# Removing the idle TensorE products ahead of the first work of an attention and MLP kernel

## The chip, the cores and the metric

The kernel runs on one core of one Trainium2 chip. A core has five engines with their own instruction streams: TensorE (PE in the profile, with its weight loads as PEld), VectorE (DVE), ScalarE (ACT), GpSimd (POOL) and SyncE (SP), which here does nothing but issue DMAs. The metric is the device time of one execution in microseconds, as the median of several runs.

## The reference

The work is attention with normed queries and keys, followed by an MLP with an unusual activation. In short:

```python
# q, k, v: (8, 12, 448, 64) float32; g_q, g_k: (64,)
q_n, k_n = rmsnorm(q, g_q), rmsnorm(k, g_k)       # x / sqrt(mean(x*x) + 1e-6) * g
scores = q_n @ k_n.T / sqrt(64)
attn   = softmax(scores)
x      = (attn @ v), heads side by side           # (3584, 768)
h      = x @ w_in                                 # w_in  (768, 2048), float64
out    = (h - tanh(h)) @ w_out                    # w_out (2048, 768), float64
```

The weights come in as float64; the kernel reads them as pairs of 32-bit words and rounds them to float32 itself.

## The kernel before, in words

**Attention in steps.** A step is one batch and one pair of heads, so there are 8 x 6 = 48 steps. For a step, `load` fetches q, k and v; `squares` (ACT, L137 and L138) squares q and k; `norm` (L147 to L149) sums the squares on DVE and takes the power -1/2 on POOL; `norm_q` (L428, DVE) scales q; `turn` (L434 to L452) transposes the keys on TensorE (L439), copies them out with the gain `g_col` to `kT` (L441, ACT), transposes the normed queries (L445) and copies them to `qT` (L449, ACT). `scores` (L518) multiplies kT by qT in blocks of 32 keys (L532), and ACT takes the exponential (L538) with the key's norm as its scale. `totals` (L654) sums the probabilities, `last_values` and `values` (L581, L631) multiply them by v, and `divide` (L706) divides. Queries and keys of a step are held in two buffers each, so the load of step s+2 waits until step s has been read: the q load for `norm_q`, the k load for the key transposes.

**The stages are laid out as a pipeline by hand.** `first_slot(s)` (L971) issues one slot: for step s the totals, values and division, for step s+1 the scores, for step s+2 the transposes, for step s+3 the squares and norms, and the load of step s+4. It runs for s from -3 to 5, so the first slots have only the front part of the pipeline. The schedule is manual: each engine works strictly in the order in which the program issues, and waits by semaphores where an operand is not there. The slots after that (`early_slot`, `slot`) mix attention with products of the MLP of an earlier batch.

**The weights.** Each slot also handles a piece of the weights: a DMA of 768 KB (`weight_load`, L279 and L283) into a staging area, two ACT operations (L71, L72), three on DVE (L78, L79, L82) and one on POOL (L90); later the pieces are combined on DVE (L342). MLP products (L761) work on two halves in each dimension with seven products in place of eight; for the first batch the second layer is done plainly (L926). All DMAs but two go through SP's queue, in program order.

**The score banks.** In the first slots five PSUM banks called `sc` are used in turn for scores and query transposes, and three called `mm` for the rest.

**The idle products.** `keep_busy` (L128 to L132) issues a number of matmuls of the identity by half of itself, into a PSUM bank that nobody reads. It is called three times at the very start: 12 products once the identity is made (L1401), 18 between the key transposes and the query transposes of step 0 (L443), and 5 after the query transposes of step 0 (L451). The profile shows each product as two matmul records and two weight loads, under L132.

Of the kernel before, what the change touches and what calls it, by code (L numbers as in the profile page):

```python
# [9 lines left out]
F32 = mybir.dt.float32  # L10
# [5 lines left out]
PSUM = bass.MemoryType.PSUM  # L16
# [76 lines left out]
def fetch(nc, name, t, pair, in_order=False):  # L93

    S = pair.shape[1]
    P = 128
    KF, KR = S // P, S % P
    if name == "q":
        if in_order:
            for h in range(2):  # L100
                nc.sync.dma_start(out=t[:, h], in_=pair[h].rearrange("(c p) d -> p c d", c=NCH))
            return
        nc.sync.dma_start(
            out=t.rearrange("p h c d -> p h (c d)"), in_=pair.rearrange("h (p c) d -> p h (c d)", c=NCH)
        )
        return
    full, rest = pair[:, : KF * P].rearrange("h (p c) d -> h p c d", c=KF), pair[:, KF * P :]
    if name == "v":
        last = t[:, :, KF]
    elif in_order:  # L110
        last = t[:, KF]
    if in_order:
        for h in range(2):
            to = t[:, h, :KF] if name == "v" else t[:, :KF, h]
            nc.sync.dma_start(out=to, in_=pair[h, : KF * P].rearrange("(c p) d -> p c d", p=P))
    elif name == "v":
        nc.sync.dma_start(
            out=t[:, :, :KF].rearrange("p h c d -> p h (c d)"), in_=full.rearrange("h p c d -> p h (c d)")
        )
    else:  # L120
        last = t[:, KF]
        for h in range(2):
            nc.sync.dma_start(out=t[:, :KF, h], in_=full[h])
    for r in range(2):
        nc.sync.dma_start(out=last[r * KR : (r + 1) * KR], in_=rest.rearrange("h p d -> p h d"))


def keep_busy(nc, ident, bank, count):  # L128

    half = ident.shape[0] // 2  # L130
    for _ in range(count):
        nc.tensor.matmul(bank[:, 512 - half :], lhsT=ident, rhs=ident[:, :half], start=True, stop=True)  # L132


def squares_of(nc, sq, n, q, k):

    nc.scalar.activation(n.rearrange("p c h d -> p (c h) d"), q.rearrange("p a b d -> p (a b) d"), AF.Square)  # L137
    nc.scalar.activation(sq, k.rearrange("p a b d -> p (a b) d"), AF.Square)  # L138


def norm_of(nc, rr, sq, n, neg_half):

    D = sq.shape[2]
    for i, x in ((1, n.rearrange("p c h d -> p (c h) d")), (0, sq)):
        rows = x.shape[0]
        r = rr[:rows, i]
        nc.vector.reduce_sum(r, x, axis=AX.X)  # L147
        nc.vector.tensor_scalar(out=r, in0=r, scalar1=1.0 / D, scalar2=1e-6, op0=ALU.mult, op1=ALU.add)  # L148
        nc.gpsimd.tensor_tensor(out=r, in0=r, in1=neg_half[:rows], op=ALU.pow)  # L149


def bounded_path(tc, ctx, q, k, v, moe_w_in, moe_w_out, out, g_col, ident, ones, half_ones, neg_half, early):
# [17 lines left out]
    nc = tc.nc  # L170
    B, H, S, D = q.shape
    DFF, DM = moe_w_out.shape
    P = 128
# [35 lines left out]
    banks = {name: [ps.tile([P, 512], F32, name=f"{name}{i}") for i in range(n)] for name, n in (("sc", 5), ("mm", 3))}  # L209
# [224 lines left out]
    def turn(s, tk, tq):  # L434

        rr, n = normed.pop(s), early["n"]
        kn = loaded.pop(("k", s))
        for c in range(NCH):
            nc.tensor.transpose(tk[:, c * P : (c + 1) * P], kn[:, c].rearrange("p h d -> p (h d)"), ident)  # L439
        kT = qkp.tile([P, S], F32, name="kT")  # L440
        nc.scalar.mul(kT, tk[:, :S], g_col)  # L441
        if s == 0:
            keep_busy(nc, ident, banks["mm"][0], 18)  # L443
        for c in range(NCH):
            nc.tensor.transpose(  # L445
                tq[:, c * CP : (c + 1) * CP], n[:, c].rearrange("p h d -> p (h d)"), ident[:CP, :CP]
            )
        qT = qkp.tile([P, S], F32, name="qT")
        nc.scalar.copy(out=qT, in_=tq[:, :S])  # L449
        if s == 0:  # L450
            keep_busy(nc, ident, banks["mm"][0], 5)  # L451
        turned[s] = rr, kT, qT  # L452


# [516 lines left out]
    def first_slot(s):  # L971
# [4 lines left out]
        if has(s + 2):  # L976
            turn(s + 2, mm_bank(), sc_bank())
# [61 lines left out]
    def slot(s):  # L1039
# [24 lines left out]
        if blocks:  # L1064
            norm_blocks(s + 2)
        elif has(s + 2):
            turn(s + 2, sc_bank(), sc_bank())
# [276 lines left out]
@with_exitstack  # L1344
def kernel(
    ctx: ExitStack,
    tc: tile.TileContext,
    q: bass.AP,
    k: bass.AP,
    v: bass.AP,  # L1350
    g_q: bass.AP,
    g_k: bass.AP,
    moe_w_in: bass.AP,
    moe_w_out: bass.AP,
    out: bass.AP,
):

    nc = tc.nc
    B, H, S, D = q.shape
    P = 128
    CP = S // NCH
    scale = 1.0 / float(D) ** 0.5

    consts = ctx.enter_context(tc.tile_pool(name="consts", bufs=1))

    rows = consts.tile([P, 4 * NCH * D], F32, name="rows")  # L1370
    early = {
        "q": rows[:CP, 2 * NCH * D :].rearrange("p (h c d) -> p h c d", h=2, c=NCH),
        "k": rows[:, : 2 * NCH * D].rearrange("p (c h d) -> p c h d", c=NCH, h=2),
        "sum": rows[:, : 2 * S].rearrange("p (h s) -> p h s", h=2),
        "n": consts.tile([CP, NCH, 2, D], F32, name="n"),
        "sq": consts.tile([P, 2 * NCH, D], F32, name="sq"),
        "rr": consts.tile([P, 2, 2 * NCH], F32, name="rr"),
    }
    gcol = consts.tile([D, 2], F32, name="gcol")
    most = consts.tile([1, 1], F32, name="most")  # L1380
    flag = consts.tile([1, 1], I32, name="flag")
    warm = consts.tile([1, 1], F32, name="warm")
    g_col = consts.tile([P, 1], F32, name="g_col")
    ident = consts.tile([P, P], F32, name="ident")
    ones = consts.tile([P, D // 2], F32, name="ones")
    half_ones = consts.tile([P, 2, D // 2], F32, name="half_ones")
    neg_half = consts.tile([P, 2 * NCH], F32, name="neg_half")
    with tc.manual_schedule(), tc.tile_pool(name="g", bufs=1) as gp:
        grow = gp.tile([1, 2, D], F32, name="grow")
        prod = gp.tile([1, D], F32, name="prod")  # L1390
        nc.scalar.dma_start(out=grow[:, 0, :], in_=g_q[None, :])
        nc.scalar.dma_start(out=grow[:, 1, :], in_=g_k[None, :])
        for name, src in (("q", q), ("k", k)):
            fetch(nc, name, early[name], src[0, 0:2])
        for i, src in enumerate((g_q, g_k)):
            nc.sync.dma_start(out=gcol[:, i : i + 1], in_=src[:, None])
        nc.vector.memset(warm, 0.0)
        nc.scalar.activation(warm, warm, AF.Exp)
        make_identity(nc, ident)
        with tc.tile_pool(name="idle", bufs=1, space=PSUM) as idle:  # L1400
            keep_busy(nc, ident, idle.tile([P, 512], F32, name="idle"), 12)  # L1401
        nc.vector.memset(neg_half, -0.5)
        nc.vector.memset(ones, 1.0)
        nc.vector.memset(half_ones, 0.0)
        for i in range(2):
            nc.vector.memset(half_ones[i * D : (i + 1) * D, i], 1.0)
        nc.vector.tensor_tensor(out=prod, in0=grow[:, 0, :], in1=grow[:, 1, :], op=ALU.mult)
        nc.vector.tensor_tensor(out=prod, in0=prod, in1=prod, op=ALU.mult)
        nc.vector.tensor_reduce(out=most, in_=prod, op=ALU.max, axis=AX.X)
        nc.vector.tensor_scalar(  # L1410
            out=flag, in0=most, scalar1=(SCORE_MAX / (scale * D)) ** 2, scalar2=None, op0=ALU.is_le
        )
        squares_of(nc, early["sq"], early["n"], early["q"], early["k"])
        norm_of(nc, early["rr"], early["sq"], early["n"], neg_half)
    bounded = nc.values_load(flag[0:1, 0:1])

    def make_g_col():
        for base in (0, D):
            nc.vector.tensor_scalar(
                out=g_col[base : base + D], in0=gcol[:, 0:1], scalar1=gcol[:, 1:2], scalar2=scale,  # L1420
                op0=ALU.mult, op1=ALU.mult,
            )

    early["g_col"] = make_g_col
    with tc.If(bounded) as cmp:
        with ExitStack() as arm, tc.manual_schedule():
            bounded_path(tc, arm, q, k, v, moe_w_in, moe_w_out, out, g_col, ident, ones, half_ones, neg_half, early)
    with cmp.Else():
        with ExitStack() as arm:
            make_g_col()  # L1430
            general_path(tc, arm, q, k, v, moe_w_in, moe_w_out, out, g_col, ident, neg_half)
# [30 lines left out]
```

## Time and profile before

| What | Value |
|---|---|
| Runs | 1392.99, 1393.02, 1395.43 us; median 1393.02 |
| Profiled execution, its own time | 1394.76 us |
| Its span in the trace | 1392.9 us |
| PE busy | 1366.8 us (98%) |
| PE weight loads busy | 1142.7 us (82%) |
| DVE busy | 942.1 us (68%) |
| POOL busy | 562.1 us (40%) |
| ACT busy | 504.3 us (36%) |
| DMA moved | 249.91 MB, 179 GB/s on average |
| L132 records on PE | 24 into the bank `idle`, 46 into the bank `mm` |

The span is the time from the first to the last instruction in the trace; the execution's own time also holds what lies around it. A row of the timeline gives start and length in us, the engine, the line of the program, the operation, and what it writes and reads; in brackets stands how long the engine was idle before it and who released it. Matmuls overlap, so the length of one record is longer than the step from one to the next. A share of busy time is an average over stages with different limits.

### The profile page before, as it was taken

How to read it: one execution, taken by the hardware profiler on the slowest of the kernel's cores; microseconds unless marked ns; L12 is line 12 of the kernel's file. 1: busy time of each engine (PE TensorE's matmuls, PEld its weight loads, DVE VectorE, ACT ScalarE, POOL GpSimd, SP SyncE). 2: the span in 40 equal slices, each digit the busy share in tenths (PEclk: the TensorE clock that was granted, in tenths of full speed). 3: DMA queues.
4: the chain of work that ended last, by engine and by line, in shares of the span. 5: the costliest groups of instructions: out<-in, count | busy, mean ns of one | idle time of the engine just before them, and what ended most of it. 6: DMA issues, size and time to landing. Idle time of an engine off the chain costs nothing.

```text
span 1392.9 us, 30057 instructions
## 1 busy us (share of the span) xinstructions
PE 1366.8 (98%) x11910; PEld 1142.7 (82%) x11910; DVE 942.1 (68%) x1545; ACT 504.3 (36%) x1147; POOL 562.1 (40%) x345
## 2 busy tenths in 40 slices
PE   9979899999999999999999999999999999999997
PEld 6458764478898898889889988988988998899997
DVE  3999978856876688567866668657885677633311
ACT  5855555233422433334332343224333234301100
POOL 3656655314542346225544236423552355402300
PEclk9999999999999999999999999999999999999999
DMA  6888789857666666766666666667667666366663
GB/s 157 184 215 214 230 257 235 219 168 180 183 165 168 174 171 173 179 158 190 173 158 183 181 162 182 178 157 181 169 165 177 177 177 188 100 188 184 191 192 89
DMA packets 367657, 249.91 MB, mean 179 GB/s; under 512 B 281748, under 2 KB 309780, under 8 KB 367508
## 3 DMA queue, kind: packets, MB, share of 16 engines
q1 hardware_dynamic: 367504, 247.90, 66.7%
q8 instruction: 96, 1.57, 0.5%
q14 instruction: 53, 0.43, 0.1%
q10 hardware_dynamic: 4, 0.00, 0.0%
HBM read 214.40 MB, written 33.42 MB: 178 GB/s over the span
## 4 chain that ended last, share of the span: by engine, by line
PE 91%; DVE 5%; DMA 2%; issue 1%; ACT 1%; POOL 0%; SPq 0%; DVEq 0%; POOLq 0%; ACTq 0%
PE mm L761 66%; PE sc L532 9%; PE sc L593 6%; PE mm L926 4%; DMA w_f<-w_out 1%; PE sc L581 1%; PE sc L631 1%; DVE w_out L82 1%; DVE w_out L79 1%; PE mm L132 1%; DMA w_raw<-in_moe_w_out_dram 1%; DVE w_out L342 1%; PE mm L631 1%; DVE rs L659 1%; DVE w_out L78 0%
## 5 line engine op out<-in xcount | busy, mean ns | idle before, releaser
L761 PE MATMUL mm<-xT,w_f 128*128 128x224 f32 x1392 | 278.5, 354 | 1.7 <-DVE s L817 1.7
L761 PEld LDWEIGHTS mm<-xT,w_f 128*128 128x128 f32 x1392 | 261.3, 190 | 16.0 <-issue 10.2
L761 PEld LDWEIGHTS mm<-gT,w_f 128*128 128x128 f32 x1344 | 252.8, 190 | 12.8 <-issue 12.8
L761 PE MATMUL mm<-gT,w_f 128*128 128x224 f32 x1344 | 263.0, 354 | 0.0
L489 POOL TENSOR_TENSOR rr_mine<-rr_mine,neg_half 128x28 f32<-128x28 f32 x33 | 159.7, 4840 | 218.2 <-DVE rr_mine L488 218.2
L532 PE MATMUL sc<-qT,kT 64*32 64x448 f32 (+1 forms) x3072 | 216.8, 501 | 6.4 <-ACT p_last L538 6.1
L761 PE MATMUL mm<-tt,w_f 128*128 128x224 f32 x1044 | 208.7, 353 | 0.0
L761 PEld LDWEIGHTS mm<-tt,w_f 128*128 128x128 f32 x1044 | 197.0, 190 | 4.4 <-issue 4.4
L798 POOL TENSOR_TENSOR gT<-s,th 128x448 f32<-128x448 f32 x96 | 120.6, 1265 | 197.2 <-ACT th L797 187.8
L761 PE MATMUL mm<-tg,w_f 128*128 128x224 f32 x1008 | 197.5, 352 | 0.0
L761 PEld LDWEIGHTS mm<-tg,w_f 128*128 128x128 f32 x1008 | 190.7, 190 | 0.0
L699 DVE TENSOR_TENSOR xT<-xT,sc 128x448 f32<-128x448 f32 x35 | 21.7, 621 | 166.5 <-PE sc L532 110.8
L532 PEld LDWEIGHTS sc<-qT,kT 64*32 64x32 f32 x3072 | 71.0, 107 | 75.0 <-issue 56.2
L721 POOL TENSOR_TENSOR tt<-xT,tt 128x224 f32<-128x224 f32 x23 | 31.1, 1353 | 232.2 <-DVE xT L703 212.0
L678 ACT COPY sum_g<-sum 32x14 f32<-32x14 f32 x280 | 56.2, 201 | 186.2 <-DVE sum L670 180.4
L593 PE MATMUL sc<-p,v_nat 64*32 64x448 f32 x1120 | 110.5, 536 | 0.0
L797 ACT ACTIVATE th<-s 128x448 f32<-128x448 f32 x96 | 55.2, 575 | 112.2 <-DVE s L823 59.2
L538 ACT ACTIVATE p<-sc 128x448 f32<-128x448 f32 x132 | 71.7, 543 | 51.7 <-PE sc L532 39.1
L926 PE MATMUL mm<-gT,w_out 128*128 128x448 f32 x192 | 74.6, 543 | 0.3 <-POOL w_out L90 0.3
L926 PEld LDWEIGHTS mm<-gT,w_out 128*128 128x128 f32 x192 | 35.7, 190 | 37.3 <-issue 35.2
L593 PEld LDWEIGHTS sc<-p,v_nat 64*32 64x32 f32 x1120 | 40.6, 107 | 31.0 <-issue 31.0
L149 POOL TENSOR_TENSOR rr<-rr,neg_half 112x8 f32<-112x8 f32 (+1 forms) x30 | 49.1, 1660 | 40.0 <-DVE rr L148 39.9
(155 smaller groups left out, 1861.1 us busy)
## 6 DMA issues: line engine op xcount, KB each, us to landing
w_f<-w_in SPq DMA_DIRECT2D x196, 384.0 KB, 3.4
w_f<-w_out SPq DMA_DIRECT2D x147, 512.0 KB, 4.2
w_raw<-in_moe_w_out_dram SPq DMA_DIRECT2D x16, 768.0 KB, 5.3
out_dram<-th SPq DMA_DIRECT2D x192, 56.0 KB, 1.9
w_in<-w_out SPq DMA_DIRECT2D x21, 384.0 KB, 6.2
qk_nat<-in_q_dram SPq DMA_DIRECT2D x132, 56.0 KB, 2.6
qk_nat<-in_k_dram SPq DMA_DIRECT2D x132, 56.0 KB, 2.6
v_nat<-in_v_dram SPq DMA_DIRECT2D x72, 96.0 KB, 3.6
```

The source lines that it names most:

```text
L149: nc.gpsimd.tensor_tensor(out=r, in0=r, in1=neg_half[:rows], op=ALU.pow)
L489: nc.gpsimd.tensor_tensor(out=mine, in0=mine, in1=neg_half[:, :1].to_broadcast([P, 2 * NJ]), op=ALU.pow)
L532: nc.tensor.matmul(tiles[h][i * BL : (i + 1) * BL, :n], lhsT=kT[r, c * P + at : c * P + at + BL], rhs=qT[r, first : first + n], start=True ...
L538: nc.scalar.activation(p[:, h, c if c < 2 else 0, :], tiles[h][:, :n], AF.Exp, scale=1.0 if rr is None else rr[:, 0, 2 * c + h : 2 * c + h ...
L593: nc.tensor.matmul(av[g][i * BL : (i + 1) * BL, :S], lhsT=v_nat[keys, h, c, m * BL : (m + 1) * BL], rhs=p[keys, h], start=first, stop=True ...
L631: nc.tensor.matmul(av[n][r : r + BL, :HS], lhsT=v_nat[:, h, c, m * BL : (m + 1) * BL], rhs=p[c][:, h, n * HS : (n + 1) * HS], start=False, ...
L678: nc.scalar.copy(out=acc[h * BL : (h + 1) * BL, g], in_=part[g * BL : (g + 1) * BL, h * NJ : (h + 1) * NJ])
L721: eng.tensor_tensor(out=t2, in0=x22, in1=t1, op=ALU.subtract)
L761: nc.tensor.matmul(bank[:, f * HS : (f + 1) * HS], lhsT=w[:, c * width + f, :], rhs=moving[p](c), start=(first and f == 0 and c == 0), sto ...
L797: nc.scalar.activation(th, h, AF.Tanh, bias=0.0, scale=1.0)
L798: eng.tensor_tensor(out=g[:, rows, cols], in0=h, in1=th, op=ALU.subtract)
L926: nc.tensor.matmul(bank[:, :S], lhsT=w_out_row(f, n // HC)[:, n % HC * P : (n % HC + 1) * P], rhs=g[:, f, :], start=(f == 0), stop=(f == C ...
```

## The change

The function `keep_busy` and its three calls are removed. Everything else stays as it is: the order of the other instructions on every engine, the tiles, the DMAs, one weight piece per slot, and the values of the third key chunk first in a slot.

```diff
-def keep_busy(nc, ident, bank, count):
-
-    half = ident.shape[0] // 2
-    for _ in range(count):
-        nc.tensor.matmul(bank[:, 512 - half :], lhsT=ident, rhs=ident[:, :half], start=True, stop=True)
...
         nc.scalar.mul(kT, tk[:, :S], g_col)
-        if s == 0:
-            keep_busy(nc, ident, banks["mm"][0], 18)
         for c in range(NCH):
             nc.tensor.transpose(
                 tq[:, c * CP : (c + 1) * CP], n[:, c].rearrange("p h d -> p (h d)"), ident[:CP, :CP]
             )
         qT = qkp.tile([P, S], F32, name="qT")
         nc.scalar.copy(out=qT, in_=tq[:, :S])
-        if s == 0:
-            keep_busy(nc, ident, banks["mm"][0], 5)
         turned[s] = rr, kT, qT
...
         make_identity(nc, ident)
-        with tc.tile_pool(name="idle", bufs=1, space=PSUM) as idle:
-            keep_busy(nc, ident, idle.tile([P, 512], F32, name="idle"), 12)
         nc.vector.memset(neg_half, -0.5)
```

## The prediction

> **What bounds the kernel now.** I read the page's busy shares first, then the chain of waits over the first 30 us, the timelines of DVE, ACT and SP there, the durations of TensorE's instructions by line, and last the chain from 58 to 260 us, to see whether an earlier start can live to the end.
>
> ```profile
> PE 1366.8 (98%) x11910; PEld 1142.7 (82%) x11910; DVE 942.1 (68%) x1545; ACT 504.3 (36%) x1147; POOL 562.1 (40%) x345
> PE   9979899999999999999999999999999999999997
> DVE  3999978856876688567866668657885677633311
> ```
>
> PE is busy 98% of the span: whatever is won must be won where PE does work nobody needs, or waits. The removed products are PE work nobody needs, so they count as "busy" here. From the sixth slice on PE alone stays at nine tenths, so a shift that survives the first 260 us should survive to the end. The chain at the start:
>
> ```profile
> 1.35 5.40 PE idle L132 x24
> 6.75 0.04 issue
> 6.80 1.11 PE mm L439 x4
> 7.91 7.57 PE mm L132 x36
> 15.48 0.75 PE sc L445 x4
> 16.23 2.05 PE mm L132 x10
> 18.28 1.79 PE sc L532 x16
> ```
>
> The three L132 pieces (12, 18 and 5 products, two records each) take 15.0 of the first 18.3 us, and the first scores (L532) wait for all of them. PE works in order, so the question is when the other inputs were ready:
>
> ```profile
> 7.70 0.69 DVE L428 TENSOR_TENSOR n<-rows,rr 112x512 f32<-112x512 f32 x1 [0.65 <-DVE rr L148]
> 8.31 0.44 DVE L1419 TENSOR_SCALAR g_col<-gcol 64x1 f32<-64x1 f32 x2
> 8.87 0.63 ACT L441 ACTIVATE kT<-mm,g_col 128x448 f32<-128x448 f32 x1 [2.73 <-DVE g_col L1419]
> 16.27 0.53 ACT L449 COPY qT<-sc 128x448 f32<-128x448 f32 x1 [6.77 <-PE sc L445]
> 16.70 0.63 ACT L137 ACTIVATE n<-q_nat 112x512 f32<-112x512 f32 x1
> ```
>
> The normed queries n end at 8.39, kT at 9.50; then ACT stands 6.77 us until the query transposes come out, and the squares of step 1 (L137 at 16.70) stand behind them in ACT's order. The next two views are the matmul durations by line, and SP's queue with the landing of step 2's last key rows:
>
> ```profile
> L132 PE MATMUL mm<-ident x7: 421/421/421, 16.6 to 17.9; 128*128 128x64 f32 x7
> L439 PE MATMUL mm<-ident,rows x4: 421/421/474, 6.8 to 7.5; 128*128 128x128 f32 x4
> L532 PE MATMUL sc<-qT,kT x32: 951/951/952, 18.2 to 20.5; 64*32 64x448 f32 x32
> L439 PE MATMUL mm<-ident,k_nat x4: 272/272/331, 21.4 to 21.8; 128*128 128x128 f32 x4
> ```
>
> ```profile
> L125 SPq DMA_DIRECT2D k_nat<-in_k_dram x1: 617/617/617, 13.5 to 13.5; - x1
> DMA to landing us min/median/max: 3.6/3.6/3.6
> 16.39 2.01 SPq L279 DMA_DIRECT2D gT<-in_moe_w_in_dram  x4
> 20.78 0.31 SPq L103 DMA_DIRECT2D q_nat<-in_q_dram  x1
> 22.12 1.24 SPq L123 DMA_DIRECT2D k_nat<-in_k_dram  x2
> ```
>
> The same transpose takes 421 ns at 7 us and 272 ns at 21.4 us, and a 448-wide score record 951 ns before 21 us and 536 ns (median) after. So TensorE ran slow until about 21.3 us, although the granted-clock column prints 1.00 there; where they differ, I go by durations.
>
> **The change, part by part.**
>
> *The first 12 products* (1.35 to 6.75). Behind them stand the key transposes. Their rows have landed by 5.50 (ACT's squares L138 start then), so the transposes start at about 5.5 instead of 6.80. Worth nothing by itself: kT waits for g_col until 8.87 in either case.
>
> *The 18 products* (7.57 us). Without them the query transposes start when n is there: 8.39 plus 0.1. At the slow rate they take 0.95 (their timeline row), so they end at 9.45; ACT finishes kT at 9.50 and copies qT by 10.04. *The 5 products* (2.05 us) stood between those transposes and the scores; now the scores start at about 10.1 instead of 18.2. That is 8.1 us at PE.
>
> What is late next? The path leaves PE. Step by step, each against its own time before:
> - Squares of step 1 on ACT at 9.9 instead of 16.70 (its query rows are there: issued at 6.05, typical landing 2.9). From that row to the normed n took 3.3 us (16.70 to 20.00), of which 1.66 is POOL's power (L149). So n of step 1 at 13.2 instead of 20.00: 6.8 us.
> - Scores of step 0 end 3.17 us after their start (18.21 to 21.38), at 13.3; key transposes at the slow rate to 14.2; query transposes, for which n is then ready (13.9), to 15.1. ACT's four exponentials (0.58 each) end by 14.5, kT and qT of step 1 by 15.7, instead of 23.65.
> - Squares of step 2 on ACT need rows that SP issued from 11.10 to 14.14. SP waited for nothing up to 18.40, so these landings do not move: the last at 13.52 + 3.6 = 17.1, the query rows ahead of them at about 16.4 (the first key rows landed 5.0 after 11.6). The key squares, at 24.05 before, start at 17.2: 6.8 us. The query squares (23.52) start at 16.4: 7.1 us.
> - From there ACT runs without a gap until 33 us, so its work, and with it the exponentials that free the score banks, is 6.7 us earlier. From 28 to 70 us PE has no gap in its timeline.
>
> *SP's queue.* It was late by two waits only: L103 at 20.78 for n of step 1 (2.38 us after the queue came free at 18.40), and L123 at 22.12 for the key transposes (1.0 us). Both go, so the queue moves by 3.4 us, not by 6.7, and from 21 to 62 us it issues almost without a pause. Are loads then late? Key rows landed ahead of their squares by 4.6 us (34.88 against 39.45), 4.0 (44.13; 48.10) and 2.85 (53.94; 56.79). With 3.4 added the tightest allows 6.25; the 0.45 us over lies inside the 1.1 us that ACT waits at 58.1 for scores. Weight pieces have 9 us in hand at their ACT step (23.2 against 34.3), values more. So 6.7 us stands. From 59 to 99 us the chain is DVE alone, fed by the slots before it, and SP's weight loads there wait for POOL (L279, 8.9 us at the longest): they follow the compute. The w_raw transfer on the chain at 165.8 is likewise released by POOL. I let the shift pass whole.
>
> [...] The rows say that 17 us of products ran at 421 ns to the last, and that the rate rose about 3.1 us after dense scores began. [...]
>
> **Sum:** 6.7 - 0.7 = 6.0 us. The profiled execution took 1394.76 (span 1392.9 and 1.9 around it), so 1388.8 against its own time; the runs' median is 1393.02, hence 1387.0. Later, the clock records fall to half at 99.8 us (3.4 us long) and 171.5 (6.8 us); shifted work may meet them otherwise, by about 2 us either way.
>
> **Rivals.**
>
> *A. The forecast,* 1387.0; own range 1384 to 1390. Chance 0.60.
>
> *B. The loads become the bound.* SP moves by 3.4 us only, and its issues are near gapless from 21 to 62 us. If slack in landings is less than I read (denser traffic, later landing), the slots move by 3.4 at most and lose some of it to the clock: about 1390. For: DMA share 0.8 to 1.0 in many stretches. Against: 2.85 to 4.6 us in hand. Chance 0.20.
>
> [...] Chance 0.08.
>
> *D. Nothing arrives.* A later wait that does not move (the DVE stretch or the w_raw transfer) gives the start back: 1392. Against: both are released by compute. Chance 0.08.
>
> *E. More than 7.5 us,* if a later half-rate stretch also goes: 1384. Chance 0.04.
>
> **How the numbers follow.** The likeliest time is A's. A change of 0.2% (2.8 us) is about what can be told from none. Faster: A 0.57, B 0.12, E 0.04, together 0.73. Within: A 0.03, B 0.08, D 0.07, 0.18. Slower: C and a remainder of D, 0.09. The range from 1383.0 to 1393.0 takes in A, B and E with the later half-rate stretches and most of D.
>
> **What would show it.** Right: no L132 rows; first L532 at about 10; ACT's qT wait gone; L103 for step 3 at 18.4; the first slot's value products (L654 at 28.19) near 21.5. Wrong: score records of 951 ns beyond 25 us (C); ACT squares waiting on k_nat in the slots around 45 to 57 us (B); DVE at the end of its stretch (99.54) no earlier (D).

## The result, and the profile after

| Kernel | Median, us | Lowest to highest | Runs |
|---|---|---|---|
| before | 1393.84 | 1392.99 to 1396.10 | 11 |
| after | 1390.36 | 1388.37 to 1391.89 | 11 |

The ratio is 0.9973, with a 95% interval of 0.9964 to 0.9983: 3.5 us faster, with 6.0 forecast. The profiled execution of after took 1391.42 us, with a span of 1389.6. The line numbers of after lie lower because lines are gone: scores L532 is L521, totals L654 is L643, the exponential L538 is L527.

The first views are timelines over the start: TensorE of after, TensorE of before, ACT of after.

```profile
8.59 0.98 PE L436 MATMUL sc<-ident,n 112*128 112x112 f32 x4 [2.14 <-DVE g_col L1406]
10.19 2.91 PE L521 MATMUL sc<-qT,kT 64*32 64x448 f32 x32 [0.62 <-ACT qT L440]
14.68 2.07 PE L521 MATMUL sc<-qT,kT 64*32 64x224 f32 x34
18.54 2.60 PE L521 MATMUL sc<-qT,kT 64*32 64x448 f32 x30 [1.79 <-ACT p_last L527]
22.86 0.96 PE L643 MATMUL mm<-p,ones 128*32 128x224 f32 x16
```

```profile
18.21 3.24 PE L532 MATMUL sc<-qT,kT 64*32 64x448 f32 x32
25.09 1.84 PE L532 MATMUL sc<-qT,kT 64*32 64x448 f32 x30 [0.45 <-ACT p_last L538]
28.19 0.97 PE L654 MATMUL mm<-p,ones 128*32 128x224 f32 x16
```

```profile
9.61 0.53 ACT L440 COPY qT<-sc 128x448 f32<-128x448 f32 x1
16.67 0.63 ACT L130 ACTIVATE n<-q_nat 112x512 f32<-112x512 f32 x1 [1.35 <-DMA q_nat<-in_q_dram]
17.52 0.63 ACT L131 ACTIVATE sq<-k_nat 128x512 f32<-128x512 f32 x1 [0.22 <-DMA k_nat<-in_k_dram]
25.38 0.63 ACT L131 ACTIVATE sq<-k_nat 128x512 f32<-128x512 f32 x1 [0.35 <-DMA k_nat<-in_k_dram]
```

Scores start at 10.19 instead of 18.21, 8.0 us earlier. Then ACT waits for step 2's rows at 16.67 and 17.52, where the prediction had them (16.4 and 17.2), and PE waits 1.79 us behind it. By the first totals (22.86 against 28.19) the lead is 5.3 us; by lead I mean how much earlier than in before the same work starts. The scores at 18.54 take 2.60 us for 30 records where before took 1.84: PE ran at half its rate. The next view of stretches of after shows it: start and end, length, then busy time and instructions of PE, PEld, DVE, ACT and POOL, then the granted clock, the DMA share and GB/s. In what follows, the gate is what switches PE's clock between full (1.00) and half (0.50), and a half-rate window is a stretch at 0.50.

```profile
12.70:19.40 6.70, 4.42 (x67) 1.83 (x59) 2.36 (x5) 5.13 (x12) 3.30 (x3) 1.00 0.94 217
19.50:22.85 3.35, 3.35 (x26) 1.63 (x21) 0.69 (x1) 3.35 (x6) 2.04 (x2) 0.50 1.08 237
166.30:173.00 6.70, 5.71 (x25) 3.90 (x26) 2.62 (x6) 2.43 (x5) 1.85 (x1) 0.50 0.92 335
238.00:241.30 3.30, 3.30 (x11) 1.47 (x5) 3.18 (x6) 1.16 (x2) 3.14 (x3) 0.50 0.75 170
```

I matched every matmul of after with the same one of before by its place in PE's order. By the times of before, as for every lead below, the lead is 5.8 us from 32 to 70 us, 5.7 at 165, 5.0 at 172, 5.14 from 185 to 236, and 2.78 from 244 to the last matmul (the spans, 1392.9 and 1389.6, differ by another half a microsecond, in what follows it). So nothing is lost in the long stretch; almost all of the loss behind the start falls at two waits, in the timeline of after and then of before:

```profile
167.29 1.74 PE L521 MATMUL sc<-qT,kT 64*32 64x448 f32 x14 [4.95 <-ACT p_last L527]
237.38 1.29 PE L521 MATMUL sc<-qT,kT 64*32 64x448 f32 x14 [2.05 <-ACT p_last L527]
```

```profile
172.31 1.74 PE L532 MATMUL sc<-qT,kT 64*32 64x448 f32 x14 [4.26 <-ACT p_last L538]
241.81 0.98 PE L532 MATMUL sc<-qT,kT 64*32 64x448 f32 x14 [1.34 <-ACT p_last L538]
```

The waits themselves grew by 0.69 and 0.71 us. Behind the second, after ran at half rate for 3.4 us and before did not (1.29 against 0.98 for the same 14 records); that took the other 1.65 us. Behind the first, both ran at half rate for 6.8 us.

PE waits there for exponentials (`p_last`), and they stand in ACT's order behind a weight piece that has yet to land. ACT at the two places, in after and then in before:

```profile
165.21 0.90 ACT L71 ACTIVATE w_out<-w_raw 128x768 f32<-128x768 f32 x1 [5.88 <-DMA w_raw<-in_moe_w_out_dram]
166.82 0.76 ACT L527 ACTIVATE p_last<-sc,rr 128x224 f32<-128x224 f32 x2
234.88 0.89 ACT L71 ACTIVATE w_out<-w_raw 128x768 f32<-128x768 f32 x1 [6.38 <-DMA w_raw<-in_moe_w_out_dram]
236.88 0.79 ACT L527 ACTIVATE p_last<-sc,rr 128x224 f32<-128x224 f32 x2
```

```profile
170.22 0.91 ACT L71 ACTIVATE w_out<-w_raw 128x768 f32<-128x768 f32 x1 [5.18 <-DMA w_raw<-in_moe_w_out_dram]
239.31 0.91 ACT L71 ACTIVATE w_out<-w_raw 128x768 f32<-128x768 f32 x1 [5.68 <-DMA w_raw<-in_moe_w_out_dram]
```

### The profile page after: what moved, and what is told of

Its sections match the earlier page's. It is cut to its first block, busy times and chain, and to the rows that moved or that the text cites. A ratio compares the mean times of both kernels' runs of the same rounds, so it can differ in the third digit from the quotient of the medians.

```text
span 1389.6 us, 29917 instructions
## 1 busy us (share of the span) xinstructions
PE 1354.1 (97%) x11840; PEld 1128.4 (81%) x11840; DVE 941.0 (68%) x1545; ACT 504.7 (36%) x1147; POOL 561.8 (40%) x345
## 4 chain that ended last, share of the span: by engine, by line
PE 85%; DMA 6%; DVE 4%; SPq 2%; ACT 1%; issue 1%; POOL 1%; ACTq 0%; DVEq 0%; POOLq 0%
PE mm L750 65%; PE sc L521 8%; PE sc L582 6%; PE mm L915 4%; DMA w_raw<-in_moe_w_in_dram 2%; DMA w_f<-w_out 1%; PE sc L570 1%; DMA gT<-in_moe_w_in_dram 1%; DMA w_raw<-in_moe_w_out_dram 1%; DMA k_nat<-in_k_dram 1%; SPq L272 1%; DVE w_out L82 1%; DVE w_out L79 1%; PE sc L620 1%; DVE w_out L335 0%
## 5 line engine op out<-in xcount | busy, mean ns | idle before, releaser
L521 PE MATMUL sc<-qT,kT 64*32 64x448 f32 (+1 forms) x3072 | 217.4, 503 | 10.0 <-ACT p_last L527 9.0
L521 PEld LDWEIGHTS sc<-qT,kT 64*32 64x32 f32 x3072 | 71.1, 107 | 78.5 <-issue 56.2
L527 ACT ACTIVATE p<-sc 128x448 f32<-128x448 f32 x132 | 71.7, 543 | 51.7 <-PE sc L521 39.1
```

Source lines behind the costliest of these rows:

```text
L521: nc.tensor.matmul(tiles[h][i * BL : (i + 1) * BL, :n], lhsT=kT[r, c * P + at : c * P + at + BL], rhs=qT[r, first : first + n], start=True ...
L527: nc.scalar.activation(p[:, h, c if c < 2 else 0, :], tiles[h][:, :n], AF.Exp, scale=1.0 if rr is None else rr[:, 0, 2 * c + h : 2 * c + h ...
```

## The experiments

The theory: products cost the start their own length until the landing of step 2's rows takes over; what the start wins is partly taken back late, where PE waits and the clock gate closes. Rivals: SP's queue paces the slots; the idle products, or some of them, did help the clock; loads alone took the gain back. All ratios are to runs of before on the same chip; its medians on the three chips were 1394.01, 1393.97 and 1393.73 us. Each kernel has one trace, which need not show its median execution.

**Only the 18 products removed**

```diff
         nc.scalar.mul(kT, tk[:, :S], g_col)
-        if s == 0:
-            keep_busy(nc, ident, banks["mm"][0], 18)
```

> Before with the 18 products alone removed; the 12 and the 5 stay. My theory: the products stood on the path one for one until the landing of step 2's rows (16.4 and 17.2 us) took over. The 5 products delay the scores by about 2.1 us (start near 12.2 instead of 10.2), but the wait for the rows absorbs that, so the first totals (L654 in before) come near 23 us, as with all products gone, and the time is 3.0 to 4.0 us under before. Rival, no wait takes over and each product costs its own length: 2.1 us slower than with all gone, about 1.4 us under before.

Measured: 1388.78, ratio 0.9960 (0.9946 to 0.9973), 5.2 us under before; the interval does not exclude the ratio of after. The timeline of PE:

```profile
9.26 2.26 PE L132 MATMUL mm<-ident 128*128 128x64 f32 x10
11.45 3.24 PE L530 MATMUL sc<-qT,kT 64*32 64x448 f32 x32
16.41 3.92 PE L530 MATMUL sc<-qT,kT 64*32 64x224 f32 x64
21.60 0.96 PE L652 MATMUL mm<-p,ones 128*32 128x224 f32 x16
```

The scores start 1.3 us later than in after, and yet the totals come at 21.60, 6.6 us before those of before. The wait for rows absorbed the 5 products, as expected, and each product does not cost its own length there. No half-rate window follows the start in this trace (four transposes at 20.26 take 0.66 us, 1.11 at 21.07 in after), which is why its totals come earlier than after's. It did better than my 3 to 4 us. If it is faster than after at all, which the interval leaves open, after's loss is not in the removal as such.

**Only the first 12 removed**

```diff
-        with tc.tile_pool(name="idle", bufs=1, space=PSUM) as idle:
-            keep_busy(nc, ident, idle.tile([P, 512], F32, name="idle"), 12)
```

> Before with the first 12 products alone removed. My theory: the key transposes start 1.4 us earlier and wait for nothing, but kT waits for g_col until 8.87 in either case and the 18 products then run from about 6.5 instead of 7.7: since they are PE's own time, everything behind them comes 1.3 us earlier (scores near 16.9), so 0.8 to 1.3 us under before, unless the products warm nothing and the rows take over. Rival, the first 12 are what opens the clock gate later: scores at half rate for longer and a time above before by about 1.5 us.

Measured: 1392.59, ratio 0.9989 (0.9980 to 0.9998), 1.4 us under before; the scores start at 16.46, 1.75 earlier. The rival's slower start did not come: the 12 warm nothing. With the other products kept, they lie on the path; the prediction's "worth nothing by itself" holds where the 18 are gone as well (the query transposes start at 8.70 with the 12 kept and the 18 gone, at 8.59 in after).

**Step 2's rows ahead of the first weight piece**

```diff
     load(1, "qk")
+    load(2, "qk")
     weight_load(0)
...
-        if s > -3:
+        if s > -2:
             load(s + 4, "qk")
```

> After with the loads of step 2's query and key rows issued ahead of the first weight piece instead of behind it. My theory (the rows' landing is what the start now waits for): the rows land near 13.5, ACT's waits at 16.67 and 17.52 go, the first totals (L643 at 22.86 in after) come 1 to 1.5 us earlier, and the time is about 1 us under after, 1389. If the half-rate clock window at 19.5 is caused by PE waiting for those rows, it goes too and another 1.4 us with it. Rival (SP's queue as a whole paces the slots): nothing moves, 1390.4.

Measured: 1389.42, ratio 0.9971 (0.9960 to 0.9983): not to be told from after. The totals come at 20.11, 8.1 us before those of before, so the rows' landing was indeed the start's limit. Then the next loads are late, in the timeline of ACT:

```profile
18.97 0.91 ACT L71 ACTIVATE w_out<-gT 128x768 f32<-128x768 f32 x1 [0.63 <-DMA gT<-in_moe_w_in_dram]
24.54 0.63 ACT L130 ACTIVATE n<-q_nat 112x512 f32<-112x512 f32 x1 [0.82 <-DMA q_nat<-in_q_dram]
25.59 0.63 ACT L131 ACTIVATE sq<-k_nat 128x512 f32<-128x512 f32 x1 [0.42 <-DMA k_nat<-in_k_dram]
33.68 0.63 ACT L131 ACTIVATE sq<-k_nat 128x512 f32<-128x512 f32 x1 [0.55 <-DMA k_nat<-in_k_dram]
```

At 42 us the lead has shrunk to 7.0, at 68 us to 6.65. Rival B of the prediction is right as a ceiling: loads hold the lead of the first slots to about 6.6 us, not to 3.4. At the end of this trace 5.9 is left, since no half-rate window follows the wait at 235 here (mean clock 0.996, 0.992 in the profiled execution of after); the other executions reach up to 1392.17.

**The start's wait filled with dense products**

```diff
         if has(s + 1):
             scores(s + 1, 2)
+        if s == -1:
+            for _ in range(2):
+                nc.tensor.matmul(banks["mm"][0][:, :S], lhsT=ident, rhs=turned[0][2], start=True, stop=True)
```

> After with two dense products (128 by 128 weights, 448 columns, into a bank that is written again before it is read) put where PE waited from 16.75 to 18.54. My theory: the half-rate clock window from 19.47 to 22.89 comes from that wait; with the array busy there the records stay at the full rate (score records 536 ns, not 951, behind 19.5), the totals come 1.2 to 1.5 us earlier than 22.86, and the time is about 1.3 us under after. Rival (only the rows' landing counts, and the clock window is chance): no change, or 0.3 us slower for the two products' own time.

Measured: 1390.36, ratio 0.9973 (0.9962 to 0.9984). In the profile the totals are 6.9 us before those of before, and no half-rate window follows the start, but the time is that of after. The profiled execution is the slowest of the seven (span 1391.7, mean clock 0.992): the wait at 234.5 grew to 3.20 us and two windows (6.8 us) at half rate followed. There a better start was given back, at the same place. The rival stands for the time.

**The late waits filled**

```diff
         divide(s, values(s, av))
+        for _ in range({8: 5, 10: 2}.get(s, 0)):
+            nc.tensor.matmul(
+                banks["sc"][(turns["sc"] + 1) % 5][:, :S], lhsT=ident, rhs=turned[s + 1][2], start=True, stop=True
+            )
         if has(s + 1):
             scores(s + 1, 2)
```

> After with dense products (128 by 128 weights, 448 columns) where PE waits for the exponential late in the first batch: 5 in the slot of step 8 (the wait of 4.95 us at 162), 2 in the slot of step 10 (the wait of 2.05 us at 235), into a score bank that the next scores overwrite. My theory: half-rate clock windows, set off by PE's waits, took back what the start had won. With the waits filled, the windows at 166 (6.8 us) and 238 (3.4 us) stay away; they cost up to half their length, so 2 to 4.5 us under after, 1386 to 1388. Rival (the loads alone took the gain back; the half-rate windows lie beside other waits): within 0.7 us of after, 1390.4.

Measured: 1386.62 (1386.08 to 1387.03), ratio 0.9943 (0.9930 to 0.9957): 3.7 us under after (4.2 by the ratios to before), 7.4 under before, and all five runs lie within 1 us. Each product shows as two records, under L1022. PE's timeline, and the stretches:

```profile
160.45 4.03 PE L1022 MATMUL sc<-qT,ident 128*128 128x448 f32 x10
165.89 0.98 PE L521 MATMUL sc<-qT,kT 64*32 64x448 f32 x14 [0.54 <-ACT p_last L527]
230.19 1.77 PE L1022 MATMUL sc<-qT,ident 128*128 128x448 f32 x4
233.61 0.98 PE L521 MATMUL sc<-qT,kT 64*32 64x448 f32 x14 [0.78 <-ACT p_last L527]
```

```profile
167.00:172.00 5.00, 5.00 (x27) 5.00 (x27) 1.50 (x4) 2.16 (x4) 0.95 (x1) 1.00 1.00 388
232.00:238.00 6.00, 5.22 (x25) 2.02 (x25) 5.67 (x10) 3.06 (x6) 3.61 (x3) 1.00 0.86 224
```

The products free no bank (PE still waits 0.54 and 0.78 us for ACT behind them), but both stretches run at clock 1.00, and the 14 scores take 0.98 us in place of 1.74 and 1.29. What this work on nothing changes there is the clock. In the two traces the first place is worth 3.2 us against after and the second 1.2; another 1.0 us comes from the start, where this execution has no half-rate window. The loads alone did not take the gain back.

**The same fills, products kept**

The edit is the last one, made to before.

> Before, idle products kept, with the fills of the two late waits (5 dense products in the slot of step 8, 2 in that of step 10). My theory: the removal moves the start by 5.5 to 6.6 us and lets late half-rate windows take back what the before kernel mostly did not lose. With the late waits filled in both kernels the removal is worth its full start gain: this one 5.3 to 6.5 us over the fills without products (1386.6), that is 1392 to 1393, and 1 to 2 us under before. Rival (the late windows cost both kernels alike, and the start gain was never more than 3.5): 1390.1, 3.5 us over the fills without products.

Measured: 1391.51, ratio 0.9985 (0.9976 to 0.9994), 2.2 us under before. So the fills give 2.2 us with the products and 3.7 without: before lost at the first wait too, and the difference of 1.5 us (2.4 by the ratios to before) is an estimate of what the late waits took from the removal over the runs. Between the two kernels with fills the removal is worth 4.9 us by their medians and 5.9 by their ratios to before, against 6.0 in the two traces (a lead of 8.2 less 2.2). Most of the start gain was there all along; the result is nearer to my theory than to 3.5, with about 2 us of uncertainty.

**The same fills with step 2's rows first, and with all three fills**

> The same fills of the waits at 162 and 235 together with step 2's rows ahead of the first weight piece. My theory: the two add, since one acts at the start and the other late: 1 us under the fills alone, 1385 to 1387. Rival: no better than rows first alone, 1389.4.

> After with all three fills, the two products at the start's wait and the fills of the two late waits. My theory: the half-rate window that may follow the start's wait of 1.8 us (19.5 in after) is kept away in every execution, so up to 1.4 us under the late fills alone where that window came, and a median 0.3 to 1 us under 1386.6. Rival (that window is rare with the late fills in): 1386.6 within 0.4.

Measured: 1387.37, ratio 0.9950 (0.9936 to 0.9964), and 1386.47, ratio 0.9948 (0.9934 to 0.9961). Neither adds to the late fills: I was wrong on both. The first has its totals 8.07 us early and, held by the loads, has 6.25 at 140 us, where the late fills have 6.66. The second says that the half-rate window at 19.5 in after's profile is no regular loss: the late fills alone, with a start wait of 1.63 us, ran through it at the full rate (30 score records in 1.84 us, 2.60 in after).

**Wide idle products**

```diff
-    half = ident.shape[0] // 2
+    n = ident.shape[0]
     for _ in range(count):
-        nc.tensor.matmul(bank[:, 512 - half :], lhsT=ident, rhs=ident[:, :half], start=True, stop=True)
+        nc.tensor.matmul(
+            bank[:, : 3 * n].rearrange("p (a b) -> p a b", a=3), lhsT=ident,
+            rhs=ident[:, None, :].to_broadcast([n, 3, n]), start=True, stop=True,
+        )
```

with counts 4, 6 and 2 in place of 12, 18 and 5.

> Before with the idle products made wide: 384 columns in place of 64, and 4, 6 and 2 of them in place of 12, 18 and 5, which at the half rate fill about the same time (1.3 us each). My theory: the narrow products never opened the clock gate because loading weights left the array half empty; wide ones open it within 3.4 to 7 us, the later products then run twice as fast, the scores start near 14 instead of 18.2 and at the full rate (536 ns), and the time is 2 to 4 us under before, but no better than after. Rival (idle products of any shape do not count, only real scores do): records at half rate until behind the first scores, scores near 18, time as before within 0.7 us.

Measured: 1392.28 (1389.33 to 1395.37), ratio 0.9988 (0.9979 to 0.9997). By line, L132's records, and PE's timeline:

```profile
L132 PE MATMUL mm<-ident x16: 486/486/502, 6.2 to 11.5; 128*128 128x384 f32 x16
L132 PE MATMUL idle<-ident x8: 486/736/1009, 1.4 to 5.2; 128*128 128x384 f32 x8
11.88 1.73 PE L535 MATMUL sc<-qT,kT 64*32 64x448 f32 x32
20.94 0.96 PE L657 MATMUL mm<-p,ones 128*32 128x224 f32 x16
236.32 1.69 PE L535 MATMUL sc<-qT,kT 64*32 64x448 f32 x14 [2.27 <-ACT p_last L541]
```

Wide products do open the gate, within their first eight records (1.36 to 5.67 us): records fall from 1009 to 486 ns, and the first scores take 1.73 us instead of 3.24. That is the width at work; why width counts, which my theory put down to weight loads (333 ns beside each record of 421 in before), was not tested. The totals are 7.25 us early, more than in after, and still only 1.7 us came of it by the medians. In the profiled execution, one of the faster ones, 3.8 us is left, and half-rate windows follow the waits at 161 (5.23 us) and 234 (2.27 us).

**36 products instead of 18**

```diff
-            keep_busy(nc, ident, banks["mm"][0], 18)
+            keep_busy(nc, ident, banks["mm"][0], 36)
```

> Before with 36 products instead of 18 between the key and the query transposes of step 0. My theory (the products are on the path, one for one): 7.6 us later from the scores on, and since the rows have long landed nothing takes over: 7 to 8 us above before, 1401.5. Rival (the late load waits and their half-rate windows give or take what the start does, as they took 2 of 5.5 us after the removal): 4 to 6 us above before.

Measured: 1400.90, ratio 1.0044 (1.0030 to 1.0058), 6.9 us above before by the medians, against 7 to 8 expected; scores start at 25.90, 7.69 later, one for one. Of that 6.1 us is left at the end of the trace. The theory stands at the start, and the rival is off by about a microsecond.

## Why the prediction was right or wrong

**Right: what the products did.** Scores at 10.19 (10.1 forecast), ACT's wait for qT gone, n and kT of step 0 where they were, rows of step 2 as the next limit. The narrow products never opened the gate in 16.6 us (421 ns to the last record), so by durations nothing was lost with them: 64 columns wide they warmed nothing, and 384 columns wide they opened the gate within 4.3 us (1.36 to 5.67).

**Right: the size of the shift.** 6.7 us was forecast without the clock. The late-fill kernel, whose start is that of after, has 6.6 at 42 us with no half-rate window. In the rows-first kernel the loads brought a lead of 8.1 down to 6.65, as the slack of 6.25 and the 0.45 us over it suggested. Two readings were off and nothing hung on them: the weight pieces had 11.1 us in hand by the prediction's own two times, not 9, and L654 at 28.19 is the totals, not value products (21.5 forecast, 22.86 in after, 21.18 in the late-fill kernel).

**Right in size by luck: the clock at the start,** 0.7 in the sum. That was an estimate of mine, and no run shows the term by itself. In after the gate opened at 12.65, under the first scores, and what cost time was that it closed again for 3.4 us at 19.47, behind PE's wait for the rows. That took 1.7 us at the first totals (a lead of 5.3, against 7.0 in the late-fill kernel), of which a wait gave some back: from 32 us on it is 0.9 (5.8 against 6.6). It differs from execution to execution, and over the runs it does not show: filling it changed nothing.

**Wrong: "I let the shift pass whole."** This is the step that failed. I read that the late w_raw waits are released by compute and concluded that they move with it. They do move, but not whole: each grew by 0.7 us, and the price of a wait is not its length alone, for the second grew from 1.34 to 2.05 us and 3.4 us at half rate now followed it. Those two waits took 2.9 us, of 5.7, in the profile, and by the runs with fills I estimate 1.5 to 2.4. The prediction had named the half-rate stretches as "about 2 us either way" and put them into the range only. They were not symmetric: the mean clock granted in the runs of before is mostly 0.995 or 0.996, which over 1393 us is 11 to 14 us at half rate; in ten of the eleven of after it is 0.992 or 0.993, some 19 to 22 us.

**The rivals.** B is right as a limit and wrong in its number. Its sign came, since ACT waits 0.60 us for key rows at 51.76 in after, but PE's lead stayed at 5.8 there. C, score records of 951 ns beyond 25 us, did not come: from 24.7 to 61.4 us they take 561 ns at most in after. Half rate does cost, but late, for one window of 3.4 us more than in before, and at the start for one at most. D, that a later wait gives the start back, came true for near half of the gain.

**Left open: why the waits grew.** The profiles show how. At the first, the piece was issued 5.71 us earlier (165.76 and 160.05, two pieces in each), as much as PE was, and ACT took it up 5.01 earlier: it took 0.7 us longer to land. At the second it shows in SP's queue, of before and then of after:

```profile
231.79 1.25 SPq L125 DMA_DIRECT2D v_nat<-in_v_dram  x2
234.32 0.46 SPq L283 DMA_DIRECT2D w_raw<-in_moe_w_out_dram  x1
```

```profile
226.55 1.83 SPq L125 DMA_DIRECT2D v_nat<-in_v_dram  x2
229.65 0.47 SPq L276 DMA_DIRECT2D w_raw<-in_moe_w_out_dram  x1
```

The value rows ahead of it took 0.6 us longer to issue, so the weight piece went out 4.67 us earlier where PE was 5.14 earlier, and ACT took it up 4.4 us earlier. The wait there was 1.34 before, 1.13 with the 12 gone, 1.14 with 36 products and 1.47 with the 18 gone, but 2.05, 2.10, 2.27 and 3.20 in after and in the kernels with rows first, wide products and the start filled. An earlier start alone does not do it: without the 18 the lead there was 7.1, more than after's 5.1. With one trace each, chance is not excluded. Nor was it tried to put ACT's exponentials ahead of the weight piece, which might take these waits away and not only fill them.

## What to carry to other kernels

Filler products ahead of the first work did harm here because the first work was ready, and the narrow ones did no good; look at the matmul durations, not at the busy share or at the clock column ahead of its first record, which prints 1.00 where score records take 951 ns. When a start is moved, check every later wait of TensorE, and the clock behind it: a wait that grew by 0.7 us, to 2.05, cost 2.4 here, since 3.4 us at half rate followed it. Dense filler in such waits, where PE stands idle anyway, paid: 3.7 us for seven products, and an execution time that repeated within 1 us.

## What the runs showed of the hardware

The half-rate stretches in the clock records are 3.41 or 6.83 us long, but for the last, which runs past the end: 99.85 to 103.27 and 171.53 to 178.36 in before; 19.47 to 22.89, 94.57 to 97.98, 166.24 to 173.07 and 237.92 to 241.34 in after.

Not every product opens the gate. Narrow ones left it shut for 16.6 us (421 ns to the last record in before), and 36 in place of 18 left it shut too (the 32 scores behind them take 3.24 us, as in before); 384-column products opened it within 4.3 us of their start (records of 1009, then 486 ns). Scores opened it 2.5 us after their start in after (10.19 to 12.65), 3.1 us in before (18.21 to 21.35) and by 4.1 us with 36 products (scores at 25.90; four transposes take 0.55 us at 29.95 in place of 0.95 at 22.96). With the products kept and the late waits filled it took longer: 4.1 us after the scores at 18.22, at 22.30, four transposes still took 0.92 us.

Half rate followed some waits of PE and not others, and the length alone does not tell which. In after it followed 1.79 us of idle ahead of 18.54, 2.54 ahead of 93.69 and 2.05 ahead of 237.38, but not 1.80 ahead of 67.07; in before it followed 2.54 ahead of 99.58, but not 1.94 ahead of 72.97. What decides is open.

At the second wait this reads as follows. Behind 2.05 us of idle in after, 2.27 with wide products and 1.47 without the 18 products, the 14 scores took 1.29, 1.69 and 1.61 us; behind 1.34 in before, 1.13 with the 12 gone and 1.14 with 36 products they took 0.98, the time at the full rate. The rows-first kernel's wait of 2.10 us was not followed by half rate (mean clock 0.996). That is how a loss of 0.7 us became 2.4 in the trace of after, and why it need not do so in every execution.
